# Two more pairs of heads turned by the matrix engine, and the wide buffers started later

## The chip, the cores and the metric

The kernel runs on one core of one Trainium2 chip. The metric is the device time of one execution in microseconds (us), the median of three runs. The profile shows one execution on the hardware profiler's clock; its span, from the first instruction to the last, is a little shorter than the device time of the same execution.

## The reference

Block-sparse attention over 4 batches of 8 heads, 768 positions, head size 64, and then an MLP mixer over its output. All inputs are float32.

```python
def _attn_ref(q, k, v, sampled_blocks):          # q, k, v: (4, 8, 768, 64)
    scores = np.matmul(q, k.transpose(0, 1, 3, 2)) / np.sqrt(D)
    # mask, in blocks of 32: the diagonal and one block either side, the first and last
    # block row and column, and three sampled blocks per row of blocks
    ...
    scores = np.where(mask, scores, -1000000000.0)
    attn = softmax(scores)                        # written out in the reference
    return np.matmul(attn, v)

def _moe_ref(x, w_tok1, w_tok2, w_ch1, w_ch2):    # x: (4, 768, 512)
    xt = x.transpose(0, 2, 1)
    h = np.maximum(xt @ w_tok1, 0.0) @ w_tok2     # (768, 256), (256, 768)
    u = x + h.transpose(0, 2, 1)
    h2 = np.maximum(u @ w_ch1, 0.0) @ w_ch2       # (512, 1536), (1536, 512)
    return u + h2
```

## The kernel before, in words

The 32 heads are worked through as 16 pairs, 0 to 15. Four pairs make one batch. Each pair goes through these steps.

- Three loads (L235, issued by GpSimd, converting to bf16 on the way) bring k, q and v of the pair into `kraw`, `qraw` and `vraw`. There are four buffers of each, so the load for pair p + 4 waits until the raw tiles of pair p have been copied on. VectorE copies v into `vaug` (L528).
- k and q lie with positions on the partitions and must be turned, so that the head size lies on the partitions, before the scores can be made. There are two ways to do this. For pairs below `NPE`, VectorE re-lays the raw tile into `klay` or `qlay` (L533), TensorE turns it with six transposes of 128 x 128 per tensor against an identity (L593), and VectorE or ScalarE evacuates the result, one head at a time, into rows 0 to 63 of `ktb` or `qtb` (L608). Rows 64 to 87 of these tiles hold the mask, as 24 extra rows of the contraction: block indicators on k's side, additive mask values on q's side. They stay in the tile from one pair to the next.
- For pairs from `NPE` on, VectorE copies the raw tile into columns 0 to 63 of `kwide` or `qwide` (L530), and SP issues one transposing DMA per tensor (L559, the crossbar), which writes all 128 rows of `ktb` or `qtb`, the mask rows included. To that end columns 64 to 127 of the wide buffers are cleared once (L496) and the mask columns are made once by twelve small matmuls `pm_wide` (L487) and copied in (L499). There are two wide buffers of each kind (`NL` = 2): the copy for pair p + 2 waits until the crossbar has read the buffer of pair p.
- There are four `ktb` and four `qtb` (`NV` = 4). A pair may be turned into its tiles when the QK matmuls of the pair four before it are done.
- For each half of the 768 query positions and each of six blocks of 128 key positions, TensorE makes the scores of both heads (QK, L639), ScalarE takes the exponential (L648), and TensorE multiplies with v (PV, L692) into `po`. At the end of a half VectorE takes the reciprocals of the row sums and scales (L706, L707) into the tile `x`.

The mixer follows per batch: the token MLP (L770, L795, with the addition L803), the turning of u (L824 and L839 by TensorE and VectorE for batch 0, L750 by the crossbar for the others), the channel MLP (L862 with the ReLU of L734 or L736, then L888), the last addition (L897, L904) and the store (L908).

The order of instructions is written by a `Planner` at build time. It holds estimated costs for TensorE, ScalarE, VectorE and SP and steps through a planned time. At each step an engine takes the ready work of the highest priority: QK first, then PV, then the turning of pairs, the token MLP, the channel MLP. Data that a DMA brings is taken to be ready at a planned landing time. `Ev(48 * US)` and the like are planned times before which a piece of work is not issued. What the planner decides is the order only: on the chip each engine runs its own list in order, and semaphores hold every instruction until its data and its buffers are there. If a buffer comes free later than planned, the instruction waits, and all that stands behind it on that engine waits with it.

The three PSUM buffers `pm` are shared by the turning, the mask matmuls and the mixer.

Of the kernel before, what the change touches and what calls it, by code (L numbers as in the profile page):

```python
# [25 lines left out]
def free(base_ap: bass.AP, extra_offset: int, dims) -> bass.AP:  # L26

    return bass.AP(
        tensor=base_ap.tensor,
        offset=base_ap.offset + extra_offset,  # L30
        ap=[list(base_ap.ap[0])] + [list(d) for d in dims],
    )
# [137 lines left out]
def kernel(  # L170
# [20 lines left out]
    NV = 4  # L191
    NR = 4
    NET = 8
    NPE = 8
    NL = 2

    sb1 = ctx.enter_context(tc.tile_pool(name="sb1", bufs=1))
# [16 lines left out]
        for n in range(NL) for nm in ("k", "q")  # L214
    }

    P = Planner({"ps": 2, "po": 1, "pm": 3, "et": NET, "a_t": 2, "o": 3, "rc": 2,
                 "uT": 3})
    US = 1e3
# [258 lines left out]
    def wide_stream():  # L478

        box, done, rel = {}, Ev(), Ev()  # L480

        def emit():
            P.take("pm", rel)
            box["m"] = psM.tile([128, 2, NC, 24], FP32, tag="pm", name="pm_wide")
            for i, rhs in enumerate((ident[R, 64:88], t2add[R, :])):
                for c in range(NC):
                    nc.tensor.matmul(  # L487
                        out=box["m"][:, i, c, :], lhsT=ind[R, c, :], rhs=rhs,
                        start=(i == 0 and c == 0), stop=(i == 1 and c == NC - 1),
                    )  # L490

        yield 500.0, [Ev(50 * US)], [("pm", 1)], emit, done
        for n in range(NL):
            for i, nm in enumerate(("k", "q")):
                def clear(eng, nm=nm, n=n):
                    nc.vector.memset(wide[nm, n][:, :, :, 64:128], 0.0)  # L496

                def copy(eng, nm=nm, n=n, i=i):
                    nc.vector.tensor_copy(  # L499
                        out=wide[nm, n][:, :, :, 64:88],  # L500
                        in_=free(box["m"][:, i, 0, :], 0, [[0, 2], [24, NC], [1, 24]]),
                    )
                ev = P.op(("dve",), {"dve": 420.0}, [Ev(48 * US)], clear, prio=6)
                ev = P.op(("dve",), {"dve": 450.0}, [done, ev], copy, prio=6)
                wide_there[nm, n].same_as = ev
                rel.same_as = ev
# [13 lines left out]
    def relayout(p):  # L520
        lays = {}
        for nm in ("k", "q", "v") if p else ("v",):
# [3 lines left out]
            def emit(eng, nm=nm, raw=raw):  # L526
                if nm == "v":
                    nc.vector.tensor_copy(out=vaug[p % NV][:, :, :, 0:64], in_=raw[:, :, :, :])  # L528
                elif p >= NPE:
                    nc.vector.tensor_copy(out=wide[nm, p % NL][:, :, :, 0:64], in_=raw[:, :, :, :])  # L530
# [8 lines left out]
            if nm == "v" and p >= NV:  # L539
                deps.append(pv_done[p - NV])  # L540
            if nm != "v" and 2 <= p < NPE:
                deps.append(qT_there[p - 1, 1])
            if nm != "v" and p >= NPE:
                deps.append(wide_there[nm, p % NL])
                if p - NL >= NPE:
                    deps.append(xb_done[nm, p - NL])
# [7 lines left out]
    def crossbar(p):  # L554

        lays = relayout(p)
        for nm, bufs, there in (("k", ktb, kT_there), ("q", qtb, qT_there)):
            def emit(eng, nm=nm, bufs=bufs):
                nc.sync.dma_start_transpose(  # L559
                    out=bufs[p % NV][:, :, :].rearrange("e h (c s) -> e (h c) s", c=NC),  # L560
                    in_=wide[nm, p % NL][:, :, :, :].rearrange("p h c e -> p (h c e)"),
                )
            deps = [lays[nm + "ev"]]
            if p >= NV:
                deps.append(qk_done[p - NV])
            ev = P.op(("sp",), {"sp": 1600.0}, deps, emit, prio=1, lat=5000.0)
            xb_done[nm, p] = ev
            there[p, 0], there[p, 1] = ev, ev

    def transposes(p):  # L570
        yield lambda: ("v", p) in raws
        if p >= NPE:
            crossbar(p)
# [52 lines left out]
    def qk_stream():  # L626
        for s in steps:
# [32 lines left out]
            else:  # L660
                deps = [e for hd in range(2) for e in (kT_there[p, hd], qT_there[p, hd])]
                if p < NPE:
                    deps.append(rows_there[p % NV])
# [273 lines left out]
    P.stream(3, tok_stream())  # L937
    P.stream(4, ch_stream())
    P.stream(-1, wide_stream())


# [55 lines left out]
```

## Time and profile before

| | |
|---|---|
| median of 3 runs | 281.69 us (279.82 to 281.86) |
| the profiled execution | 281.69 us |
| its span | 280.0 us |
| mean granted TensorE clock | 0.975 |
| PE busy | 265.3 us (95%), 2571 matmuls |
| ScalarE busy | 184.7 us (66%) |
| VectorE busy | 115.5 us (41%) |
| exponentials L648 | 192, 144.6 us |
| transposing DMAs | 8 into `ktb`, 8 into `qtb`, 6 into `uT` |
| loaded by GpSimd's queue | 12.98 MB (as written to the core) |

The profile gives busy time, waits and a chain of waits for one execution. PE is TensorE's matmuls, PEld its weight loads, DVE VectorE, ACT ScalarE, POOL GpSimd, SP the engine that issues most of the plain and all of the transposing DMAs. A "q" behind an engine's name is its instruction queue. A wait that has several causes is put down to the one that came last. PE's clock is shown as the share of full speed that was granted.

### The profile page before, as it was taken

What the parts mean: (1) busy time and instruction counts of PE and PEld (TensorE: products, weight loads), DVE (VectorE), ACT (ScalarE), POOL (GpSimd) and SP (SyncE); (2) the same over time, 40 slices, a digit from 0 to 9 for tenths busy, and PEclk for the clock granted to TensorE, in tenths of its full rate; (3) what the DMA queues carried; (4) which work ended last, traced back from release to release, by engine and by line L of the source; (5) the groups of instructions that cost most, each with busy time, mean ns of one, the idle gap of its engine ahead of it and who ended that gap; (6) DMA issues with size and microseconds to landing.
All of it is one profiled execution on the core that took longest, in us unless ns stands there. A gap on an engine that the chain in (4) does not pass through costs nothing.

```text
span 280.0 us, 6156 instructions
## 1 busy us (share of the span) xinstructions
PE 265.3 (95%) x2571; PEld 171.4 (61%) x2571; DVE 115.5 (41%) x263; ACT 184.7 (66%) x272; POOL 42.1 (15%) x66
## 2 busy tenths in 40 slices
PE   8899999982699999999999999999999999999995
PEld 3477777762377776777767766456545654456444
DVE  7878878751346365464443544200021002200022
ACT  6899999990389999999999960057302770067200
POOL 8746364640303100000000000000000000000000
PEclk9999999996589999999999999999999999999999
DMA  6999999999959978499030022420023002210123
GB/s 150 191 215 205 210 202 205 202 187 165 157 80 168 181 104 120 95 144 122 20 60 2 2 56 71 138 75 0 5 109 112 2 0 76 105 48 0 37 79 111
DMA packets 54748, 29.48 MB, mean 105 GB/s; under 512 B 35968, under 2 KB 51088, under 8 KB 54720
## 3 DMA queue, kind: packets, MB, share of 16 engines
q0 software_dynamic: 15104, 12.98, 30.1%
q1 hardware_dynamic: 39344, 15.91, 27.6%
q8 instruction: 20, 0.33, 0.5%
q10 hardware_dynamic: 272, 0.20, 0.3%
q14 instruction: 8, 0.07, 0.1%
HBM read 26.74 MB, written 6.29 MB: 118 GB/s over the span
## 4 chain that ended last, share of the span: by engine, by line
PE 79%; ACT 10%; DMA 6%; DVE 2%; issue 1%; DVEq 0%; ACTq 0%
PE pm_ch L862 22%; PE pm_ch L888 21%; PE ps L639 17%; ACT et L648 10%; PE po L692 9%; DMA qtb<-qwide 5%; PE pm_tok L770 3%; PE pm_tok L795 3%; PE ps_idle L299 2%; DMA out_dram<-o 1%; DVE qtb L402 0%; PE tk L593 0%; PE pm_e L395 0%; PE tq L593 0%; DVE qtb L388 0%
## 5 line engine op out<-in xcount | busy, mean ns | idle before, releaser
L648 ACT ACTIVATE et<-ps 128x768 bf16<-128x768 f32 x192 | 144.6, 810 | 14.5 <-PE ps L639 13.1
L639 PE MATMUL ps<-qtb,ktb 88*128 88x384 bf16 x384 | 95.9, 331 | 1.8 <-ACT et L648 1.1
L862 PE MATMUL pm_ch<-uT,w_ch 128*128 128x384 bf16 x384 | 73.0, 326 | 2.3 <-DVE uT L839 2.3
L734 ACT ACTIVATE rc<-pm_ch 128x384 bf16<-128x384 f32 x72 | 35.4, 491 | 56.5 <-PE pm_ch L862 56.4
L692 PEld LDWEIGHTS <-et 128*128 128x128 bf16 x1152 | 56.6, 98 | 22.0 <-issue 1.4
L888 PE MATMUL pm_ch<-w_ch,rc 128*128 128x512 bf16 (+2 forms) x312 | 64.0, 363 | 0.0
L692 PE MATMUL po<-vaug,et 128*128 128x65 bf16 x1152 | 61.5, 194 | 0.0
L897 DVE TENSOR_TENSOR o<-pm_ch,x 128x512 f32<-128x512 f32 x23 | 15.9, 692 | 87.1 <-PE pm_ch L888 87.1
L862 PEld LDWEIGHTS <-w_ch 128*128 128x128 bf16 x384 | 36.3, 98 | 21.0 <-issue 0.2
L888 PEld LDWEIGHTS <-rc 128*128 128x128 bf16 x312 | 29.4, 98 | 31.1
L639 PEld LDWEIGHTS <-ktb 88*128 88x128 bf16 x384 | 35.8, 99 | 15.4 <-issue 5.9
L803 DVE TENSOR_TENSOR x<-pm_tok,x 128x512 bf16<-128x512 f32 x24 | 16.0, 686 | 10.2 <-PE pm_tok L795 10.2
L706 DVE RECIPROCAL recip<-po 128x6 f32<-128x6 f32 x32 | 6.2, 195 | 31.5 <-PE po L692 31.1
L736 DVE TENSOR_SCALAR rc<-pm_ch 128x384 bf16<-128x384 f32 x24 | 13.2, 555 | 13.0 <-PE pm_ch L862 13.0
L707 DVE TENSOR_TENSOR x<-po,recip 128x384 bf16<-128x384 f32 x32 | 17.8, 557 | 1.1
L770 PE MATMUL pm_tok<-x,w_tok 128*128 128x256 bf16 x96 | 17.3, 279 | 0.0
L795 PE MATMUL pm_tok<-a_t,w_tok 128*128 128x256 bf16 x96 | 16.9, 276 | 0.0
L235 POOL DMA_DIRECT2D vraw<-in_v_dram x16 | 11.6, 725 | 34.0 <-DVE vaug L528 29.9
L235 POOL DMA_DIRECT2D kraw<-in_k_dram x15 | 10.8, 719 | 7.5 <-DVE vaug L528 1.7
L235 POOL DMA_DIRECT2D qraw<-in_q_dram x15 | 10.7, 716 | 7.2 <-DVE x L803 1.9
L795 PEld LDWEIGHTS <-w_tok 128*128 128x128 bf16 x96 | 9.8, 129 | 1.4
L824 PE MATMUL pm_ut<-ident,x 128*128 128x128 bf16 x24 | 2.9, 248 | 5.9 <-DVE x L803 5.9
(73 smaller groups left out, 102.4 us busy)
## 6 DMA issues: line engine op xcount, KB each, us to landing
out_dram<-o SPq DMA_DIRECT2D x23, 256.0 KB, 2.0
vraw<-in_v_dram POOLq DMA_DIRECT2D x16, 192.0 KB, 8.7
w_ch<-in_moe_w_ch_dram POOLq DMA_DIRECT2D x8, 384.0 KB, 10.2
kraw<-in_k_dram POOLq DMA_DIRECT2D x15, 192.0 KB, 9.9
qraw<-in_q_dram POOLq DMA_DIRECT2D x15, 192.0 KB, 9.8
w_tok<-in_moe_w_tok_dram POOLq DMA_DIRECT2D x2, 384.0 KB, 9.7
kf<-in_k_dram SPq DMA_DIRECT2D x2, 192.0 KB, 3.3
ktb<-ktb SPq DMA_DIRECT2D x3, 72.0 KB
```

What stands on the lines that cost most here:

```text
L235: nc.gpsimd.dma_start(out=raw[:, :, :, :], in_=APx(src, 2 * p * S * D, [[NC * D, 128], [S * D, 2], [1, NC * D]]),)
L639: nc.tensor.matmul(out=ps[:, hd, 0:384], lhsT=ktb[n][0:88, hd, 128 * j : 128 * j + 128], rhs=qtb[n][0:88, hd, 384 * half : 384 * half + 38 ...
L648: nc.scalar.activation(out=et[:, :, :], in_=ps[:, :, 0:384], func=AF.Exp, scale=0.125)
L692: nc.tensor.matmul(out=po[:, hd, c, :], lhsT=et[:, hd, 128 * c : 128 * c + 128], rhs=va[:, hd, j, 0:65], start=(j == 0 and hd == 0 and c = ...
L707: nc.vector.tensor_tensor(out=free(xs[b][:, pb // 2, 3 * half, 128 * (pb % 2) : 128 * (pb % 2) + 128], 0, [[64, 2], [256, 3], [1, 64]],), ...
L734: nc.scalar.activation(out=o(), in_=i, func=AF.Relu)
L770: nc.tensor.matmul(out=box["pm"][:, t, :], lhsT=w_tok1[:, sc, 128 * t : 128 * t + 128], rhs=xs[b][:, g, sc, :], start=(t == 0 and sc == 0) ...
L795: nc.tensor.matmul(out=ubox["pm"][:, i, :], lhsT=w_tok2[:, t, :, 2 * s2 + i], rhs=a_t[:, t, :], start=(i == 0 and t == 0), stop=(i == 1 an ...
L803: nc.vector.tensor_tensor(out=st[b]["u"][:, g, 2 * s2 : 2 * s2 + 2, :], in0=ubox["pm"][:, :, :], in1=xs[b][:, g, 2 * s2 : 2 * s2 + 2, :], ...
L862: nc.tensor.matmul(out=pbox["pm"][:, 0:384], lhsT=w_ch1[:, dmc, 128 * cc : 128 * cc + 128], rhs=st[b]["uT"][:, dmc // 2, 3 * sh : 3 * sh + ...
L888: nc.tensor.matmul(out=pbox["pm"][:, 0:n], lhsT=box["rc"][:, cc, 128 * sc : 128 * sc + 128], rhs=w_ch2[:, cc, lo : lo + n], start=(cc == 0 ...
L897: nc.vector.tensor_tensor(out=o[:, :].rearrange("p (g e) -> p g e", g=2), in0=pbox["pm"][:, :].rearrange("p (g e) -> p g e", g=2), in1=st[ ...
```

## The change

`NPE` goes from 8 to 10: pairs 8 and 9 are turned by TensorE, as pairs 1 to 7 are, and the crossbar begins with pair 10. The planned times before which the mask matmuls `pm_wide` and the clearing of the wide buffers are not issued go from 50 and 48 us to 62 and 60 us.

```diff
@@ -191,7 +191,7 @@
     NV = 4
     NR = 4
     NET = 8
-    NPE = 8
+    NPE = 10
     NL = 2
 
@@ -489,7 +489,7 @@
                         start=(i == 0 and c == 0), stop=(i == 1 and c == NC - 1),
                     )
 
-        yield 500.0, [Ev(50 * US)], [("pm", 1)], emit, done
+        yield 500.0, [Ev(62 * US)], [("pm", 1)], emit, done
         for n in range(NL):
             for i, nm in enumerate(("k", "q")):
                 def clear(eng, nm=nm, n=n):
@@ -500,7 +500,7 @@
                         out=wide[nm, n][:, :, :, 64:88],
                         in_=free(box["m"][:, i, 0, :], 0, [[0, 2], [24, NC], [1, 24]]),
                     )
-                ev = P.op(("dve",), {"dve": 420.0}, [Ev(48 * US)], clear, prio=6)
+                ev = P.op(("dve",), {"dve": 420.0}, [Ev(60 * US)], clear, prio=6)
                 ev = P.op(("dve",), {"dve": 450.0}, [done, ev], copy, prio=6)
                 wide_there[nm, n].same_as = ev
                 rel.same_as = ev
```

The line numbers of the kernel stay as they are. What `NPE` decides is in `transposes` (`if p >= NPE: crossbar(p)`) and in `relayout`, which copies into `wide` or `lay`.

## The prediction

> **What bounds the kernel now.** I read the slices of the page first, then stretches cut to fit what they showed, then who waited for whom, then the order on SP and VectorE around the place. The slices:
>
> ```profile
> PE   8899999982699999999999999999999999999995
> PEclk9999999996589999999999999999999999999999
> DMA  6999999999959978499030022420023002210123
> ```
>
> Each digit is 7 us. PE is full everywhere except at the start, at the end and in one hole, the tenth and eleventh slice (63 to 77 us). The granted clock falls in the same place, one slice longer. The DMA engines are full up to and through the hole and not behind it. The chain that ended last is PE work for 79% of the span and exponentials for 10%, with one large foreign piece in it, "DMA qtb<-qwide 5%". So PE sets the time, and time is lost only where PE stands or runs slowly. The table by stretches, cut at the edges of the hole (columns: start:end, length, then busy time of PE, weight loads, VectorE, ScalarE, GpSimd with their counts, granted clock, DMA share, GB/s):
>
> ```profile
> 42.00:49.00 7.00, 6.92 (x104) 5.38 (x101) 6.13 (x15) 7.00 (x10) 2.91 (x5) 1.00 1.25 205
> ...
> 62.00:68.00 6.00, 0.12 (x4) 0.00 (x0) 0.96 (x2) 0.84 (x2) 0.00 (x0) 0.73 1.35 163
> 68.00:78.50 10.50, 8.21 (x63) 5.42 (x64) 2.22 (x6) 4.10 (x6) 2.14 (x3) 0.50 1.09 166
> 78.50:84.00 5.50, 5.50 (x77) 4.31 (x75) 3.04 (x7) 5.42 (x8) 0.00 (x0) 1.00 0.30 52
> ```
>
> From 62 to 68 everything stands while the DMA engines run at full share. From 68 to 78.5 PE works, with holes, at clock 0.50. The waits between 50 and 80 us:
>
> ```profile
> ACT et L648 <- PE ps L639: 11.7, 7, 6.5
> DVE kwide L530 <- DMA vraw<-in_v_dram: 7.1, 1, 7.1
> PEld L824 <- DVE x L803: 6.0, 1, 6.0
> PE pm_ut L824 <- DVE x L803: 5.9, 1, 5.9
> DVE qwide L530 <- DMA qtb<-qwide: 4.1, 1, 4.1
> PE pm_ch L862 <- DVE uT L839: 2.3, 1, 2.3
> ```
>
> ScalarE waits for PE, PE for VectorE, VectorE twice for a DMA at L530. The issues on SP give the reason (start, duration, instruction):
>
> ```profile
> 53.25 3.67 SPq L559 DMA_TRANSPOSE ktb<-kwide  x1
> 57.09 8.41 SPq L559 DMA_TRANSPOSE qtb<-qwide  x1
> 65.61 5.57 SPq L559 DMA_TRANSPOSE ktb<-kwide  x1
> 71.22 1.51 SPq L559 DMA_TRANSPOSE qtb<-qwide  x1
> 82.25 1.43 SPq L559 DMA_TRANSPOSE ktb<-kwide  x1
> ```
>
> The first two are pair 8, the next two pair 9, the last is pair 10's first. Issue to landing is 13.7 and 14.9 us for pair 8, so 66.95 and 71.96. These are the moments at which VectorE goes on (67.02 and 72.06):
>
> ```profile
> 67.02 0.36 DVE L530 COPY kwide<-kraw 128x768 bf16<-128x768 bf16 x1 [7.13 <-DMA vraw<-in_v_dram]
> ...
> 72.06 0.36 DVE L530 COPY qwide<-qraw 128x768 bf16<-128x768 bf16 x1 [4.07 <-DMA qtb<-qwide]
> ```
>
> Those two copies belong to pair 10 and overwrite the wide buffer that pair 8's transposes are still reading. The name vraw in the first row is the load that happened to land last. VectorE is in order, so an addition of L803, the uT evacuation L839 and the norms L706/L707 queue behind, and PE runs dry 2.2 us after VectorE does (59.9 to 62.1).
>
> **What the hole costs.** 16.5 us (62.0 to 78.5) hold 0.12 + 8.21 us of PE work. The 8.21 ran at clock 0.50 (two QK matmuls step 0.64 us there and 0.33 elsewhere in the chain), so they are worth 4.1 at full clock. Lost: 16.5 - 0.1 - 4.1 = 12.3 us.
>
> **The change, part by part.**
> *Pairs 8 and 9 leave the crossbar.* Gone are four transposing DMAs, the four of SP above that meet the full DMA queue. In the built order the first one left is pair 10's, behind the exponential of (pair 6, half 1, step 5); it waits for pair 6's QK to free the ktb buffer, as it did before. At ScalarE's pace (14 exponentials in 10.39 us = 0.742 us) that place is about 70 us. The loads that fill the queue are by then down to the last two pairs: the software queue's 12.98 MB at some 205 GB/s are 63 us from about 7 us on, all of it. The copy that reuses pair 10's wide buffer (pair 12) stands 9 exponentials behind pair 10's issue, about 7 us. Before, the same distance was 82.25 to 89.28 for k and 83.74 to 90.02 for q, with no wait on either. So nothing blocks VectorE: I take the whole 12.3 off. If landing takes longer than 6.3 to 7.0 us the cover is gone; landings off the full queue in this trace are 3.9 to 7.7, on it 13.7 and 14.9. I take the near end, since the DMA share falls from 1.16 to 0.43 at 74 us even with the hole in the schedule.
>
> *PE.* 2 pairs x 2 tensors x 6 = 24 transposes at L593 are added. Four of the same kind at L824 step from 61.21 to the next matmul at 61.45: 60 ns each, 1.4 us in all. PE sets the end, so they count in full.
>
> *VectorE.* Added: 8 evacuations L608 (0.555 us) = 4.4 and 4 re-layouts L533 (0.35 for k, 0.40 for q) = 1.5. Removed: 4 wide copies L530 (0.35) = 1.4. Net 4.5 us, between about 50 and 72 us; ScalarE gets none of it in the built order. The cover is VectorE's own slack: with pairs turned in just this way it was busy 6.13 of 7 us (42 to 49) while ScalarE lost nothing (7.00). Without that slack the price is up to 4.5 us. klay8 now stands where the first wide memset stood, at 50.2 us; its load was issued at 39.75 and took 11.1 us to land, so VectorE waits until about 50.9. Behind it is a_t, whose matmuls end only at about 52: free. SP's queue holds nothing else there. GpSimd's load for pair 12 waits for klay8 instead of kwide8 and goes out some 4 us earlier than its 55.25.
>
> *The later start of the wide buffers* (memsets and pm_wide gate 48/50 to 60/62 us of plan) moves 4 memsets, 4 casts and 12 matmuls and adds none. It takes a pm buffer for about 12 exponentials and so leaves PE less filler. I counted the built order: per half pair QK 12 x 0.163 and PV 36 x 0.030 = 3.04 us, plus filler. First half of pair 6: 9 transposes (0.54), 12 pm_wide (0.39), 1 ch (0.16) = 4.13. Second half: 6 transposes (0.36), 5 tok (0.55) = 3.95. ScalarE needs 6 x 0.742 = 4.45. PE idles 0.3 + 0.5 = 0.8 us there. Bounds: 0 (stretches like 56 to 62 idle 0.03) to 1.5 us (if both tensors' evacuations hold the other pm buffers too).
>
> *Sum against the profiled execution.* 280.0 - 12.3 + 1.4 + 0.8 = 269.9 us of span. That execution took 281.69 us, 1.69 more than its span, and 281.69 is also the median of the runs. So 271.6 us. A second way: 5 exponentials stand in the 15.6 us between 62.84 and 78.46, which need 3.9 at the pace behind the hole (16 in 12.46): -11.7. In the built order 305 instead of 293 L862 matmuls are left after the last QK: 12 x 0.163 = +2.0. That gives 270.3 of span, 272.0.
>
> *Two rules.* Pair 8's transposes took 13.7 and 14.9 us while plain loads issued beside them took 8.5 to 11.3. The Trainium skill, "Advanced Engine Details and Errata", section X-Bar Transpose (TRN2), says that crossbar transposes run about as fast as ordinary DMAs, at 350 to 400 GB/s. That speaks against the change: by it a 384 KB tile would be an estimated 1 us, the crossbar would have stolen nothing worth removing, and the sum would be 281.7 + 1.4 + 0.8 = 283.9. The trace's landings on a full queue decide for me. From 42 to 49 us, with transposes among the matmuls, the granted clock was 1.00. The skill's "TensorE: Matmul & The Clock Gate", Part 4, says PE transposes do not count as busy for the gate; with 24 more among hundreds of matmuls its rule costs nothing I can see either.
>
> **The rivals.**
> *A shorter wait comes back at pair 12's copies* (0.08). The changed kernel's pair 10 transposes are issued at about 70 us, with the loads of pairs 14 and 15 going out beside them. For it: those loads are 1.2 MB. Against it: in the trace the same neighbours at 85 to 87 us cost no wait. The hole cost 12.3 us for 7.1 + 4.1 = 11.2 us of blocked VectorE, 1.1 to 1. With a landing of 11.3 us (the longest plain load) the block is 11.3 - 6.3 = 5.0, the price 5.5: 277.1 us.
>
> *VectorE becomes the bound from 50 to 72 us* (0.05). For it: 86% busy in the like stretch. Against it: that stretch ran at ScalarE's full pace. All 4.5 us exposed: 276.1 us.
>
> *The clock falls anyway, or only the standing time is won* (0.05). Idle in the hole is 5.88 + 2.29 = 8.2; the half clock's 4.1 would stay: 275.7 us. Against it: no drop elsewhere from 14 to 62 us.
>
> *The whole block moves to pairs 12 and 13, slower than before* (0.04). One mechanism: VectorE blocked at L530 behind pair 10's transposes as it is now behind pair 8's. It breaks even at (281.7 - 271.6) / 1.1 = 9.2 us of block, a landing of 6.3 + 9.2 = 15.5 us, above the 14.9 seen; at 19 us the block is 12.7, the price 14.0, the time 285.6.
>
> *It does not do what it says* (0.04). The queue is jammed by the loads alone, and VectorE then waits for raw data where it waited for buffers; the time stays at 281.7 to 283.
>
> **How the numbers follow.** The forecast, stall gone, has 0.74: 271.6 us, its own range 269.4 (no added work exposed: 280.0 - 12.3 + 1.7) to 274. Reaching over the partial cases the range is 269.3 to 276.5. Faster by over 1% (below 278.9) 0.91 (the first four cases, less a hundredth for the second's far end); within 1%, about what runs spread over 279.82 to 281.86 us can tell from nothing, 0.05; slower 0.04.
>
> **What would show it.** Right: no digit below 9 in PE's slices between 14 and 260 us, PEclk without a dip, "DMA qtb<-qwide" gone from the chain, the L530 waits near nothing, 108 matmuls at L593 reading klay and qlay (84 now), 36 evacuations at L608 where there are 28. The first L559 issue near 70 us, landing within 8 us. Wrong: a hole at 70 to 85 us behind L530 (first or fourth rival), VectorE's digits at 9 with ScalarE below (second), or waits for raw loads at L533 (last).

## The result and the profile after

The changed kernel takes 271.27 us (median of 4 runs, 271.09 to 272.31) against 281.74 us before: a ratio of 0.9651, 95% interval 0.9604 to 0.9699. The forecast was 271.6. The profiled execution took 271.3 us for a span of 269.6, where the forecast had a span of 269.9. Some executions of a kernel are slower than others of the same kernel; those more than 1.5% above the fastest are left out of every ratio in this document, and the profiles of e3, e6 and e7 are of such executions.

The slices of the page after:

```profile
PE   8898999999999999999999999999999999999995
PEclk9999999999999999999999999999999999999999
DMA  6999999999799863971300036300122002310123
```

The hole at 63 to 77 us is gone, and the clock's dip with it. The DMA engines now come off full load in the eleventh slice; each slice is 6.74 us here. The stretches (start:end, length, busy time of PE, weight loads, VectorE, ScalarE, GpSimd, then clock, DMA share, GB/s), cut as before the change:

```profile
42.00:49.00 7.00, 6.92 (x112) 5.52 (x111) 6.13 (x14) 7.00 (x11) 2.86 (x4) 1.00 1.25 205
49.00:56.00 7.00, 7.00 (x99) 5.37 (x98) 4.39 (x11) 6.96 (x10) 4.30 (x6) 1.00 1.31 202
56.00:62.00 6.00, 6.00 (x86) 4.88 (x85) 4.59 (x11) 5.96 (x9) 3.06 (x4) 1.00 1.31 201
62.00:68.00 6.00, 5.79 (x89) 3.99 (x87) 5.18 (x13) 5.78 (x9) 0.72 (x1) 1.00 0.90 128
68.00:74.00 6.00, 5.99 (x83) 4.59 (x82) 5.52 (x16) 5.97 (x9) 1.79 (x3) 1.00 0.68 86
```

PE was busy 0.12 of the 6 us from 62 to 68 before, and is busy 5.79 of them now. VectorE carries more (5.18 and 5.52 of 6) and ScalarE loses next to nothing by it. Who turns the pairs is seen in the counts: the line of TensorE's turning (L593) has 54 matmuls for k and 54 for q, 42 each before, and L608 has 36 evacuations. The issues on SP, and VectorE where it reuses pair 10's wide buffers:

```profile
70.64 2.00 SPq L559 DMA_TRANSPOSE ktb<-kwide  x1
72.75 2.94 SPq L559 DMA_TRANSPOSE qtb<-qwide  x1
...
77.50 0.35 DVE L530 COPY kwide<-kraw 128x768 bf16<-128x768 bf16 x1
...
80.06 0.36 DVE L530 COPY qwide<-qraw 128x768 bf16<-128x768 bf16 x1 [0.76 <-DMA qtb<-qwide]
```

Pair 10 goes out at 70.64 and 72.75 us and lands 5.6 and 7.2 us later. The copy that reuses kwide finds it free; the one that reuses qwide waits 0.76 us. That is all that is left of the 11.2 us of waits at L530.

### The profile page after: what moved, and what is told of

Read it like the earlier page. It is cut to its first block, busy times and chain, and to the rows that moved or that the text cites. A ratio compares the mean times of both kernels' runs of the same rounds, so it can differ in the third digit from the quotient of the medians.

```text
span 269.6 us, 6198 instructions
## 1 busy us (share of the span) xinstructions
PE 262.9 (98%) x2595; PEld 170.5 (63%) x2595; DVE 118.8 (44%) x269; ACT 184.8 (69%) x274; POOL 42.2 (16%) x66
## 4 chain that ended last, share of the span: by engine, by line
PE 80%; ACT 14%; DVE 3%; issue 1%; DMA 1%; ACTq 0%; DVEq 0%
PE pm_ch L862 23%; PE pm_ch L888 22%; PE ps L639 17%; ACT et L648 14%; PE po L692 9%; PE pm_tok L795 3%; PE pm_tok L770 3%; PE ps_idle L299 2%; DMA out_dram<-o 1%; PE tk L593 1%; PE tq L593 1%; DVE ktb L608 0%; DVE qtb L402 0%; PE pm_ut L824 0%; PE pm_e L395 0%
## 5 line engine op out<-in xcount | busy, mean ns | idle before, releaser
L639 PE MATMUL ps<-qtb,ktb 88*128 88x384 bf16 x384 | 93.7, 325 | 1.7 <-ACT et L648 1.1
L734 ACT ACTIVATE rc<-pm_ch 128x384 bf16<-128x384 f32 x74 | 36.3, 491 | 59.3 <-PE pm_ch L862 43.3
L862 PE MATMUL pm_ch<-uT,w_ch 128*128 128x384 bf16 x384 | 72.2, 326 | 0.0
L692 PEld LDWEIGHTS <-et 128*128 128x128 bf16 x1152 | 55.3, 97 | 21.6 <-DVE x L707 1.5
L692 PE MATMUL po<-vaug,et 128*128 128x65 bf16 x1152 | 60.4, 193 | 0.4 <-DVE x L707 0.4
L639 PEld LDWEIGHTS <-ktb 88*128 88x128 bf16 x384 | 35.0, 98 | 11.6 <-issue 3.0
L803 DVE TENSOR_TENSOR x<-pm_tok,x 128x512 bf16<-128x512 f32 x24 | 15.9, 686 | 11.3 <-PE pm_tok L795 11.2
L736 DVE TENSOR_SCALAR rc<-pm_ch 128x384 bf16<-128x384 f32 x22 | 12.2, 553 | 12.5 <-PE pm_ch L862 12.4
L770 PE MATMUL pm_tok<-x,w_tok 128*128 128x256 bf16 x96 | 16.5, 272 | 0.0
L235 POOL DMA_DIRECT2D vraw<-in_v_dram x16 | 11.6, 725 | 18.6 <-DVE vaug L528 14.5
L608 DVE COPY ktb<-tk 64x768 bf16<-64x768 bf16 x18 | 9.9, 552 | 3.0 <-PE tk L593 2.8
```

The source lines that it names most:

```text
L235: nc.gpsimd.dma_start(out=raw[:, :, :, :], in_=APx(src, 2 * p * S * D, [[NC * D, 128], [S * D, 2], [1, NC * D]]),)
L639: nc.tensor.matmul(out=ps[:, hd, 0:384], lhsT=ktb[n][0:88, hd, 128 * j : 128 * j + 128], rhs=qtb[n][0:88, hd, 384 * half : 384 * half + 38 ...
L692: nc.tensor.matmul(out=po[:, hd, c, :], lhsT=et[:, hd, 128 * c : 128 * c + 128], rhs=va[:, hd, j, 0:65], start=(j == 0 and hd == 0 and c = ...
L734: nc.scalar.activation(out=o(), in_=i, func=AF.Relu)
L770: nc.tensor.matmul(out=box["pm"][:, t, :], lhsT=w_tok1[:, sc, 128 * t : 128 * t + 128], rhs=xs[b][:, g, sc, :], start=(t == 0 and sc == 0) ...
L803: nc.vector.tensor_tensor(out=st[b]["u"][:, g, 2 * s2 : 2 * s2 + 2, :], in0=ubox["pm"][:, :, :], in1=xs[b][:, g, 2 * s2 : 2 * s2 + 2, :], ...
```

## The experiments

The theory: pair 8's crossbar transposes land late because loads fill the DMA engines beside them; VectorE, in order, stands at the copy that reuses their wide buffer; PE runs dry behind it. The main rival: crossbar transposes cost by themselves, in proportion to their number. Every kernel below was timed beside the kernel before on the same chip; its "ratio" is its time over that one's, with the 95% interval in brackets. "L530 waits" are the times that VectorE stood at the copies into the wide buffers.

### The two parts by themselves

e1, the pairs alone:

```diff
-    NPE = 8
+    NPE = 10
```

> Pairs 8 and 9 turned by TensorE, the wide buffers' planned times left at 48 and 50 us. Theory (the two pairs' crossbar transposes on a full DMA queue blocked VectorE): the whole gain is here, 271.0 to 272.0 us, span 269.5 to 270.5, no hole in PE's slices. Rival (the later planned times let the queue drain and do part of the work): a part of the hole stays, 273 to 279 us, with a wait at L530 of several us.

Measured: 273.31 us (271.85 to 275.23), ratio 0.9706 (0.9641 to 0.9771). No hole in the tenth to twelfth slice. L530 waits 2.1 us in all. The median is over the expected range, and the profiled execution (275.23 us) shows why it is not the fault of the change: its clock dips at 10 to 18 us, where the program is still the same as in all other kernels here.

```profile
10.00:14.00 4.00, 2.79 (x27) 2.13 (x26) 2.80 (x7) 1.97 (x3) 2.43 (x4) 0.57 1.27 191
14.00:18.00 4.00, 4.00 (x47) 2.85 (x44) 1.41 (x5) 2.02 (x3) 2.15 (x4) 0.58 1.13 225
```

There VectorE waited 1.2 us for pair 1's k to land, and ScalarE was busy 4.0 of these 8 us, against 7.4 in the profile of the changed kernel. Executions without that dip (mean clock 0.998 and 1.0) took 271.85 and 272.40 us. So the pairs carry the gain; by these two executions the later start adds about 1 us at most, which was not separated from the scatter.

e2, the later start alone:

```diff
-        yield 500.0, [Ev(50 * US)], [("pm", 1)], emit, done
+        yield 500.0, [Ev(62 * US)], [("pm", 1)], emit, done
...
-                ev = P.op(("dve",), {"dve": 420.0}, [Ev(48 * US)], clear, prio=6)
+                ev = P.op(("dve",), {"dve": 420.0}, [Ev(60 * US)], clear, prio=6)
```

> The planned times at 60 and 62 us, all pairs from 8 on still by the crossbar. In the built order pair 8's wide copies go from (pair 5, step 0) to (pair 6, half 1, step 0), about 66 us, when the loads issued so far have landed. Theory (what costs is a transpose that meets a full queue while VectorE's next copy stands behind it, not the crossbar as such): landings fall from 14 to 4 to 10 us, VectorE is blocked 0 to 4 us, 269.5 to 273.5 us, since no TensorE transposes are added. Rival (only taking the pairs off the crossbar helps): as before, 280 to 284 us, with L530 waits of 10 us or more.

Measured: 287.28 us (284.15 to 287.79), ratio 1.016 (1.0083 to 1.0237). The expectation was wrong, and on the side of the rival. The stretches of e2:

```profile
62.00:66.00 4.00, 4.00 (x64) 2.83 (x60) 3.10 (x10) 3.83 (x6) 0.00 (x0) 1.00 0.00 0
66.00:74.00 8.00, 8.00 (x109) 6.33 (x106) 5.95 (x16) 7.93 (x12) 4.31 (x6) 1.00 1.20 121
74.00:82.00 8.00, 3.55 (x42) 2.28 (x40) 0.96 (x2) 4.14 (x6) 0.72 (x1) 0.94 1.41 122
```

The queue did drain: DMA share 0.00 from 62 to 66. But the same late copies hold the raw buffers, so the loads of pairs 12 and 13 cannot go out either. They go out between 66.4 and 71.3 us, in the same moment as the transposes, which start at 66.14:

```profile
66.14 1.55 SPq L559 DMA_TRANSPOSE ktb<-kwide  x1
67.86 4.32 SPq L559 DMA_TRANSPOSE qtb<-qwide  x1
72.28 8.70 SPq L559 DMA_TRANSPOSE ktb<-kwide  x1
81.02 5.15 SPq L559 DMA_TRANSPOSE qtb<-qwide  x1
```

Landings are 8.3, 14.6 and 14.6 us for the first three. L530 waits 13.5 us for q and 6.2 for k, 19.7 in all. What follows: the backlog of older loads is not needed for the trouble. Six loads issued beside the first three transposes are enough. Together they moved 121 GB/s, where loads alone moved 205 at a like share (42 to 49 us of the changed kernel, above).

e3, one pair only:

```diff
-    NPE = 8
+    NPE = 9
```

> Only pair 8 is turned by TensorE, the planned times at 48 and 50 us; pair 9 still uses the crossbar, issued at about 61 us on a full queue, and pair 11's copies, which reuse its wide buffer, stand 9 exponentials (6.7 us) behind. Theory: landing 8 to 11 us, VectorE blocked 2 to 4 us, price 1.1 times that less PE's 2.2 us of reserve: 271.5 to 275 us. Rival (the cost goes with the number of crossbar pairs): half the gain, 276 to 277 us.

Measured: 272.12 us (271.67 to 279.44), ratio 0.9654 (0.9605 to 0.9703): the theory's range, not half the gain. Three executions took 271.67 to 272.29 us, one 279.44. The profile is of that last one and shows the old hole some 9 us later (PE runs dry at 71 us): pair 9's q was issued at 63.99 and let VectorE go on at 77.14, 13 us on, after 8.2 us of waiting.

```profile
77.14 0.36 DVE L530 COPY qwide<-qraw 128x768 bf16<-128x768 bf16 x1 [8.25 <-DMA qtb<-qwide]
```

One pair off the crossbar suffices in three executions of four; in the fourth, the profiled one, the wait was back.

### Order alone

e4 is the kernel before with the planner told a longer landing, so that pair 10's copies stand later in VectorE's order:

```diff
-            ev = P.op(("sp",), {"sp": 1600.0}, deps, emit, prio=1, lat=5000.0)
+            ev = P.op(("sp",), {"sp": 1600.0}, deps, emit, prio=1, lat=15000.0 if p < 10 else 5000.0)
```

> The kernel before with one number changed: the planner reckons 15 us instead of 5 from the end of a crossbar issue to its landing for pairs 8 and 9. The transposes of both pairs stay on the crossbar and on the full queue, with landings as before (13 to 15 us for pair 8); what moves is VectorE's order, where pair 10's copies now stand at (pair 6, half 1, step 3) and (pair 7, step 2), about 69 and 73 us. Theory (the in-order wait on VectorE is the whole cost): the L530 waits fall from 11.2 us to 0 to 2, 268.5 to 271.5 us, at or below the changed kernel as TensorE has 24 transposes less. Rival (the slow transposes themselves, or the contention of DMA, cost the time): a hole stays, 276 to 284 us.

Measured: 277.55 us (275.69 to 279.21), ratio 0.985 (0.9788 to 0.9913). Between theory and rival. Pair 10's copies wait 0.9 us instead of 11.2, as the theory said. But pair 8's and 9's transposes still took SP long to issue, so pair 10's came out late, and pair 12's copy (the first of the two in the last row) met them. SP, then VectorE:

```profile
58.10 7.72 SPq L559 DMA_TRANSPOSE qtb<-qwide  x1
65.93 7.05 SPq L559 DMA_TRANSPOSE ktb<-kwide  x1
73.03 3.71 SPq L559 DMA_TRANSPOSE qtb<-qwide  x1
76.83 2.15 SPq L559 DMA_TRANSPOSE ktb<-kwide  x1
...
84.43 0.63 DVE L530 COPY kwide<-kraw 128x768 bf16<-128x768 bf16 x2 [5.57 <-DMA ktb<-kwide]
```

"In-order VectorE is the whole cost" falls. SP is a second in-order queue: pair 9's transpose, which took 7.05 us to issue, held back the three behind it. Moving one copy moves the wait.

### What turning on TensorE costs

e5 turns pairs 8 and 9 twice (core of the edit; `start` clears, so the second round overwrites):

```diff
-            for c in range(NC):
+            turns = NC * (2 if p in (8, 9) else 1)
+            for r in range(turns):
...
+                    c = r % NC
```

a1, the changed kernel again on the same chip:

> The changed kernel once more, on the chip of the next three, so that they can be set against it: 270.5 to 272.5 us.

> The changed kernel with pairs 8 and 9 turned twice by TensorE (24 further transposes, the second round overwrites the first; nothing else is added). Theory (PE sets the end, so that its added matmuls count in full): 24 x 60 ns = 1.4 us over the changed kernel run beside it. Rival (TensorE's slack under ScalarE's pace hides them in this stretch): within 0.5 us of it.

Measured: a1 271.50 us (271.07 to 272.46), ratio 0.962 (0.9551 to 0.969). e5 273.28 us (273.00 to 273.63). The medians differ by 1.8 us, 74 ns for each of the 24 transposes; the executions of the two do not overlap. PE's busy time grows by the same 1.8 us, from 262.9 in the changed kernel's profile to 264.7. The added matmuls count in full, at a little more than the 60 ns of the step.

### The loads beside the transposes

e6 is the kernel before with the four loads of w_ch2, the channel MLP's second weights, behind pair 15's; e7 is the same edit in the changed kernel:

```diff
-        if p == 7:
+        if p == NP - 1:
             loads.append(load_ch2)
```

> The kernel before with one line changed: the four loads of w_ch2 (1.57 MB, 7.7 us of the full queue), first needed at about 164 us, go out behind pair 15's loads instead of ahead of pair 8's. The crossbar still takes pairs 8 and 9, issued at about 53 us as before, but the queue has then about 9.05 MB behind it, 44 us from 7 us on, so it is nearly empty. Theory (a full queue makes the transposes late, their lateness blocks VectorE): pair 8 lands within 5 to 9 us instead of 14, L530 waits 0 to 3 us in all, 269.5 to 273 us. Rival (the crossbar is slow by itself at that place): landings of 13 us and 280 us or more.

Measured: 274.25 us (271.21 to 276.47), ratio 0.9636 (0.9527 to 0.9744). With all pairs from 8 on still on the crossbar most of the gain is there. In the profiled execution (275.58 us) landings are 3.8 to 10.2 us, L530 waits 8.7 us in four pieces of at most 4.4, and no slice of PE after the start is under 8. The queue had drained as expected (DMA share 0.12 from 55 to 57 us), but new loads went out at 55.6, 56.3 and 57.7 us, beside pair 8's transposes (55.37 and 57.09), which landed after 8.5 and 9.1 us. The expected 0 to 3 us of waits was too little. Two executions, 271.21 and 272.93 us, are in the expected range; the profiled one, which also has the dip at the start, and one of 276.47 are above it.

> The changed kernel with the w_ch2 loads moved behind pair 15's as well. Theory (PE is full and nothing waits for DMA any more): the same as the changed kernel, 270.5 to 272 us. Rival (contention with loads still costs something spread out): 268 to 270 us.

Measured: 281.46 us (274.74 to 283.12, 10 runs); the ratio, of the three executions up to 278.31, is 0.9835 (0.9755 to 0.9915). Both theory and rival were wrong. Those three lost over half of the gain that a1 had beside them (0.962); the other seven, the profiled one of 282.0 us among them, lost nearly all of it. GpSimd, SP and VectorE in e7:

```profile
83.82 3.06 POOL L261 DMA_DIRECT2D w_ch<-in_moe_w_ch_dram  x4
...
82.16 1.46 SPq L559 DMA_TRANSPOSE ktb<-kwide  x1
83.68 3.72 SPq L559 DMA_TRANSPOSE qtb<-qwide  x1
89.12 7.06 SPq L559 DMA_TRANSPOSE ktb<-kwide  x1
...
99.20 0.36 DVE L530 COPY qwide<-qraw 128x768 bf16<-128x768 bf16 x1 [9.07 <-DMA qtb<-qwide]
```

The 1.57 MB went out at 83.8 us, beside pair 11's transposes. Pair 11's q was issued at 83.68 and let VectorE go on at 99.20, 15.5 us on, after VectorE had stood 9.1 us at pair 13's copy. PE did 1.15 us of work from 91 to 100. It is the hole of before, made again 29 us later with other pairs and other loads.

To undo this, e8 (kernel before) and e9 (changed kernel) hold the loads back on the chip with a small write that they must wait for:

```diff
+    def hold(eng):
+        nc.vector.memset(w_ch2[:, 0:12:3, 0:1], 0.0)
+        held.append(1)
+    P.op(("dve",), {"dve": 60.0}, [Ev(118 * US)], hold, prio=2)
...
+            if x is load_ch2 and not held:
+                return
```

> The kernel before, the w_ch2 loads behind pair 15's as in e6, but held back on the chip: a memset of four columns of w_ch2 by VectorE, planned at 118 us, has to run before GpSimd can issue them. So they meet neither pair 8's nor pair 11's transposes. Theory: the L530 waits of e6 near 92 us go and those near 60 us stay (e6 had 8.7 us in all), 269.5 to 272 us. Rival (the crossbar for pairs 8 and 9 is too slow even on a queue without w_ch2): 274 us or more.

Measured: 273.25 us (271.23 to 274.89), ratio 0.9676 (0.9604 to 0.9748). L530 waits 5.5 us: those before 70 us stay (4.7, e6 had 3.1), the one near 92 us falls from 4.4 to 0.9. 271.23 and 272.42 at mean clocks of 1.0 and 0.998 are in the range, the other two, at 0.988 and 0.992, above it.

> The changed kernel with the w_ch2 loads held back in the same way. Theory for the slow e7 (the w_ch2 burst, which GpSimd issued at 83.8 us, met pair 11's transposes issued at 82.2 and 83.7 us and gave the hole of before again, 31 us later): without the meeting no hole, 270.5 to 272 us. Rival (some other effect of moving the loads): 276 us or more as in e7.

Measured: 272.29 us (271.62 to 272.50), ratio 0.964 (0.958 to 0.9699), L530 waits 0.9 us. On the chip the loads went out at 120.7 us, behind pair 15's transposes (117.14 and 118.62):

```profile
120.68 3.06 POOL L261 DMA_DIRECT2D w_ch<-in_moe_w_ch_dram  x4 [36.09 <-DVE w_ch L953]
```

The same loads, out of the transposes' way, cost nothing that shows: the ratio is 0.964, a1's was 0.962. e7 against e9 shows the mechanism most plainly: apart from the small write, the two kernels differ only in when 1.57 MB are issued.

### Towards a better version

e10 is e8 with the planner told 9 us (pairs below 12) instead of 5 for the landing; e11 is e10 with `NPE = 9`.

> e8 with the planner reckoning 9 us instead of 5 from a crossbar issue to its landing for pairs 8 to 11, so that pair 10's copies stand at (pair 6, step 3) and not at (pair 5, half 1, steps 3 and 4). Theory: no wait is left at L530 (under 1 us), no transposes of pairs 8 and 9 on TensorE: 1.4 to 2 us under the changed kernel, 269 to 270.5 us. Rival (other waits take their place): 271.5 us or more.

Measured: one execution of 270.11 us with a span of 268.4, clock 1.0, no wait at L530; three others took 275.72 to 276.94, so no ratio can be given. What those three waited for is not known, as the profile is of the first.

> What the runs point to, with a safer margin than e10: pair 8 by TensorE, pair 9 by the crossbar, the w_ch2 loads held back to 118 us of plan, 9 us reckoned for the landings of pairs 9 to 11. Pair 11's copies, which reuse pair 9's wide buffer, then stand 14 exponentials (10.4 us) or more behind its issue. Theory: no wait at L530, 12 transposes less on TensorE than the changed kernel, 0.7 to 1 us under it in its undisturbed executions: 270.2 to 271.2 us. Rival (the early crossbar costs something that no wait shows): 272 us or more.

Measured: 271.04 us (270.05 to 271.67, 6 runs), ratio 0.9625 (0.9585 to 0.9665). No wait at L530, landings 3.8 to 5.2 us, span 268.2. At full clock it took 270.05 and 270.58 us where a1 took 271.07 and 271.18: the 0.7 to 1 us expected of 12 transposes less. But the intervals overlap, so that it beats the changed kernel is likely and not shown.

## Why the prediction was right, point by point

**What the hole cost.** 12.3 us were to come back. e10's and the changed kernel's spans allow a check: without any hole, 24 transposes fewer gave 268.4, where 280.0 - 12.3 is 267.7. The size holds within 0.7 us. Its two parts can be seen in PE's own time. The prediction put 8.2 us of the hole down to PE standing and 4.1 to work at half clock. From before to after, the time in which PE stands falls from 14.7 to 6.7 us of the span, by 8.0, and its busy time from 265.3 to 262.9, by 2.4, where 4.1 less the 1.8 that e5 gives for the added transposes is 2.3. So both parts came back, and the rival "only the standing time is won" falls.

**What VectorE waited for.** The last rival had it wait for raw data. Pair 10's k and q, loaded at 48.44 and 50.38 us in the kernel before, landed 8.6 and 7.6 us later, by 57.0 and 58.0 us, before the first wait at L530 began (59.9). So it waited for the wide buffers, as the prediction read it.

**The price of a blocked VectorE**, 1.1 us for each us. Each row is one profiled execution, the hole's size taken from the span of the like kernel without it (268.4 for `NPE` 8, 269.6 for 10, 270.2 as the middle of e3's others):

| | waits at L530 | hole in the span | ratio |
|---|---|---|---|
| before | 11.2 | 280.0 - 268.4 = 11.6 | 1.0 |
| e2 | 19.7 | 286.1 - 268.4 = 17.7 | 0.9 |
| e3 | 8.4 | 277.7 - 270.2 = 7.5 | 0.9 |
| e4 | 6.9 | 276.0 - 268.4 = 7.6 | 1.1 |
| e7 | 9.1 | 280.3 - 269.6 = 10.7 | 1.2 |

About one for one (e4's span also holds a dip at the start). That makes VectorE's wait a fair measure of the whole, though VectorE is busy only 41% of the span before.

**Where the first crossbar pair would be, and its cover.** Forecast 70 us, seen 70.64. The cover was said to be 6.3 to 7.0 us against landings of 3.9 to 7.7; q's landing of 7.2 met a cover of 6.55 (VectorE was ready at 79.30 for what was issued at 72.75), and 0.76 us of waiting came of it. "Nothing blocks VectorE" was true by a hair. e7 shows how little it takes.

**Why landings would be short.** This reason was incomplete. The prediction counted the backlog of loads up to about 70 us. e2, where the DMA share was 0.00 just before, and e7 show that loads issued at the same time as the transposes do the same without that backlog. In the changed kernel four loads went out from 70.4 to 75.8 us beside pair 10's transposes, where e2 had six in 5.7 us. That fewer loads in that moment made the difference is likely and was not tested by itself; the prediction's reason would not have told the two kernels apart.

**PE's added work**, 1.4 us, was too small: 1.8 us by e5. **The idle time from the pm buffers**, 0.8 us, was too large: PE idles 0.22 us in all from 62 to 74 us after the change, where pair 6 is worked on and the mask matmuls now stand. The errors, +0.4 and -0.6 us, nearly cancel, which is luck; with the measured terms, 280.0 - 12.3 + 1.8 + 0.2 is 269.7, and 269.6 was seen.

**VectorE's added 4.5 us** stayed covered: 5.52 of 6 us busy at worst, ScalarE 5.97 of 6 there. A side remark missed: GpSimd's first load for pair 12 went out at 54.90 us, 0.35 us earlier than before and not some 4, behind the loads ahead of it on GpSimd (51.96, 53.01 and 53.93).

**The rule on crossbar speed.** Pair 8's transposes, 384 KB each, landed 13.7 and 14.9 us after their issue in the kernel before; the 384 KB loads of w_ch took 10.2 us there in the median. In e11 the transpose issued at 98.20 us, on a queue with a DMA share of 0.05, landed after 3.8 us. The Trainium skill's "Advanced Engine Details and Errata", X-Bar Transpose (TRN2), says that transposes run about as fast as ordinary DMAs; these landings do not agree with that beside loads, and the 3.8 us, issue included, are more than the 1 us estimated from its rate. Why a transpose beside loads lands so late is not shown.

**Signs that were named.** One digit misses: PE's fourth slice has an 8. From 20 to 27 us PE was busy 6.17 us against 6.75 before, and VectorE waited 0.6 us each for a v and a q to land; the program is the same in both there.

## What to carry to other kernels

A transfer that lands late costs little by itself; it costs what stands behind the instruction that waits for it on an in-order engine, so look there first, and price the hole by that wait. Before moving work off a DMA queue or a load to "later", list what else is issued in that moment: the same 1.57 MB cost nothing that shows at 121 us and more than half of the change's gain at 84 us. A gate in a planner's time moves an instruction's place in its list and no more: in e7 GpSimd issued the w_ch2 loads straight behind the last load of the pairs (83.1 us), and only the small write of e9, which they had to wait for, kept them back.

## What the runs showed of the hardware

In e2 transposing DMAs mixed with loads moved 121 and 122 GB/s at a DMA share of 1.20 and 1.41, loads alone 205 at 1.25. That low rate is not general: in the hole of the kernel before the mix moved 163 GB/s from 62 to 68 us and 204 from 68 to 74, at shares of 1.35 and 1.26. The issue of one transposing DMA took SP 1.43 us at 82.25 us of the kernel before, where the DMA share was 0.30, and up to 8.70 us beside loads (e2); SP issued the next one only after it.

The granted clock in the hole of the kernel before, by one or two microseconds (columns as above):

```profile
62.00:64.00 2.00, 0.12 (x4) 0.00 (x0) 0.00 (x0) 0.84 (x2) 0.00 (x0) 1.00 1.44 192
64.00:66.00 2.00, 0.00 (x0) 0.00 (x0) 0.00 (x0) 0.00 (x0) 0.00 (x0) 0.70 1.33 106
...
73.00:74.00 1.00, 1.00 (x6) 0.44 (x6) 0.98 (x3) 0.00 (x0) 0.00 (x0) 0.50 1.16 218
...
77.00:78.00 1.00, 1.00 (x10) 0.68 (x8) 0.00 (x0) 0.81 (x1) 0.00 (x0) 0.50 1.30 195
78.00:79.00 1.00, 1.00 (x12) 0.70 (x10) 0.00 (x0) 0.54 (x1) 0.00 (x0) 0.78 1.20 170
```

A mean of 0.70 over 64 to 66 puts the fall at about 64.8 us, 2.7 us after PE stopped; 0.78 over 78 to 79 puts the rise at about 78.4, after 5.4 us of unbroken work from 73 on. The Trainium skill, "TensorE: Matmul & The Clock Gate", Part 1, has the clock change after a window of about 3.4 us of idling or of work, and has these windows run freely, whenever the work starts. The trace agrees for the rise: the 13.6 us at half clock are four such windows, and the last of them, from about 75 us on, was full of work. The fall came 2.7 us after PE stopped, sooner than a full window of idling. So a hole costs more than the time that PE stands: in this one 4.1 of 12.3 us were work at half clock.
